# Chunked delta rule and token/channel mixer on one core: inversion rounds of two and then four units, and a first batch element ordered by hand

## The chip, the cores and the metric

The kernel runs on one core of a Trainium2 chip. The metric is the device time of one execution in microseconds; three executions before the change gave 915.23, 920.13 and 922.28 us. A difference of about 1% is what such a measurement can tell from none.

## The reference

Four batch elements, eight heads, 768 time steps, head size 48. A delta rule keeps a 48 x 48 state per head; its output, heads side by side, goes through an MLP mixer over tokens and one over channels. All is float32.

```python
k_n = k / (np.linalg.norm(k, axis=-1, keepdims=True) + 1e-06)
for t in range(S):
    y[:, :, t] = np.einsum('bhd,bhde->bhe', q[:, :, t], state)
    v_old = np.einsum('bhde,bhd->bhe', state, kt)
    state = state + bt[:, :, :, None] * np.einsum('bhd,bhe->bhde', kt, vt - v_old)
...
h = np.maximum(x.transpose(0, 2, 1) @ w_tok1, 0.0) @ w_tok2      # x: (4, 768, 384)
u = x + h.transpose(0, 2, 1)
out = u + np.maximum(u @ w_ch1, 0.0) @ w_ch2
```

The inputs arrive as 64-bit floats where numpy made them so (the four weights); the kernel turns these into float32 itself.

## The kernel before, in words

**Units.** A unit is 128 time steps of one batch element, all eight heads; there are 24, six to a batch element. Inside a unit the time steps are two chunks of C = 64. For a chunk the sequential rule becomes matrix algebra: with a strictly triangular matrix N of k-products times beta, the inverse of a unit triangular 64 x 64 matrix is needed per chunk and head. A unit therefore has 16 such matrices, and each is handled as two 32 x 32 diagonal blocks and one off-diagonal block.

**The stages of a unit.** `load_kq` (L213) brings k and q. `prep` (L246) normalises k (ScalarE square L255, VectorE L257 to L271), restacks it with four transfers into kst (L278), transposes k and q on TensorE (L286, L299), spreads them into the block-diagonal kbd (ScalarE L291, GpSimd L292), multiplies p_g (L310, sixteen matmul records a unit) and masks it into gm on VectorE (L312, twice a unit); the diagonal 32 x 32 blocks then go to DRAM (L327). `invert` (L333) works on a round of RU = 2 units: it loads their 64 diagonal blocks one to a partition (L339), runs the substitution as 30 pairs of VectorE operations (L344, L348), makes a transposed copy xt on GpSimd (L355), stores both to DRAM (L358, L359) and fetches them back in the layout of matmul operands: wt (L369), w22 (L373) and t11 (L378). `join` (L384) makes the off-diagonal block with two rounds of matmuls, p_z (L392) and p_x (L403). `recur` (L412) is one chunk of the recurrence, a step: p_q (L427), r_bd on VectorE (L429, two operations), p_w (L442), w_bd on ScalarE (L446), p_s (L451), the state s_bd on VectorE (L455, two operations) and the output chunk y (L433, L461). The state chains one step to the next; a batch element has twelve steps.

**The mixer.** `mixer` (L468) of a batch element needs all six units of it, as the token MLP sums over time: p_1 (L475), then p_h (L487), and then per 128 time steps p_c (L513) and p_o (L528) of the channel MLP. TensorE is free to work on the next batch element's units between these.

**The weights.** `round_weights` (L159) takes a piece of up to 384 columns: one load of 64-bit words (L168), two ScalarE operations (L174, L175), two integer VectorE operations (L176, L180), one on GpSimd (L184), and one on VectorE (L186) for the result. There are 34 pieces: ten of w1 and w2, then twelve each of wc1 and wc2. `beta` is read with sixteen small transfers (L144) and transposed.

**Order.** Nothing is written out by hand: each stage is a generator, `at(time, dt, fn, ...)` (L544) gives it a due time and a step, in units of one unit's work, and `run_plan` (L547) calls the generators in the order of due times. That order is a priority: the scheduler that builds each engine's fixed instruction list may put an operation that it expects to be ready ahead of an older one that it expects to wait. Each engine then runs its own list strictly in order. All transfers are issued from SyncE's queue, also in order.

```python
at(t0 - 2.9 + j, 0.08, prep, u)
if j == 0:
    at(t0 - 1.4, 0.9 / (HB + 2), invert, rnd)
at(t0 - 0.4 + 0.2 * j, 0.1, join, u)
for cc in range(2):
    at(u + 0.5 * cc, 0.15, recur, 2 * u + cc)
if c == NCH - 1:
    at(u + 1, NCH / (n_mixer + 1), mixer, b)
```

The functions, with the line numbers of the profile:

## Time and profile before

| | |
|---|---|
| median of three runs | 920.13 us (915.23 to 922.28) |
| profiled execution | 917.84 us, span 916.1 us, granted TensorE clock 0.901 in the mean |
| busy share of the span | PE 80%, PE weight load 65%, VectorE 52%, ScalarE 25%, GpSimd 15% |
| transfers | 56.06 MB, 28.8% of 16 engines' span on the one queue that carries them |

All times in rows are of the one profiled execution. PE is TensorE's matmuls and PEld its weight loads, DVE is VectorE, ACT ScalarE, POOL GpSimd, SP SyncE and SPq its queue of transfers. A granted clock of 1 is 2.4 GHz, of 0.5 is 1.2 GHz. A float32 matmul of the program appears as two matmul records.

### The profile page before, as it was taken

How to read it: one execution, taken by the hardware profiler on the slowest of the kernel's cores; microseconds unless marked ns; L12 is line 12 of the kernel's file. 1: busy time of each engine (PE TensorE's matmuls, PEld its weight loads, DVE VectorE, ACT ScalarE, POOL GpSimd, SP SyncE). 2: the span in 40 equal slices, each digit the busy share in tenths (PEclk: the TensorE clock that was granted, in tenths of full speed). 3: DMA queues.
4: the chain of work that ended last, by engine and by line, in shares of the span. 5: the costliest groups of instructions: out<-in, count | busy, mean ns of one | idle time of the engine just before them, and what ended most of it. 6: DMA issues, size and time to landing. Idle time of an engine off the chain costs nothing.

```text
span 916.1 us, 13640 instructions
## 1 busy us (share of the span) xinstructions
PE 735.6 (80%) x5034; PEld 594.5 (65%) x5034; DVE 473.3 (52%) x1254; ACT 232.5 (25%) x535; POOL 138.3 (15%) x150
## 2 busy tenths in 40 slices
PE   3301820660889999999899999998999999799998
PEld 2301710540758878877688788786888787567876
DVE  5696499285274491763835918548358174210000
ACT  3322523320311412313124133041241321211110
POOL 7433225120110100201101012011011000000000
PEclk9555875695699999999999999999999999989999
DMA  5655444431232322413223234232230212000000
GB/s 105 139 134 121 92 110 134 99 74 37 41 61 44 66 49 55 95 44 63 59 56 60 42 74 79 48 73 41 56 67 21 50 38 54 11 1 9 18 9 18
DMA packets 192354, 56.06 MB, mean 61 GB/s; under 512 B 182560, under 2 KB 185632, under 8 KB 192288
## 3 DMA queue, kind: packets, MB, share of 16 engines
q1 hardware_dynamic: 192288, 55.19, 28.8%
q8 instruction: 40, 0.66, 0.3%
q14 instruction: 26, 0.21, 0.1%
HBM read 36.27 MB, written 14.16 MB: 55 GB/s over the span
## 4 chain that ended last, share of the span: by engine, by line
PE 58%; DVE 19%; DMA 7%; ACT 5%; issue 4%; POOL 3%; SPq 3%; POOLq 0%; ACTq 0%; DVEq 0%
PE p_c L513 14%; PE p_o L528 13%; DVE x L348 6%; DVE sub L344 6%; PE p_s L451 6%; PE p_q L427 4%; PE p_w L442 4%; PE p_h L487 4%; PE p_g L310 3%; PE p_z L392 3%; PE p L475 3%; PE p_x L403 3%; ACT w_bd L446 3%; DMA t_dram<-xt 2%; DMA t<-t_dram 1%
## 5 line engine op out<-in xcount | busy, mean ns | idle before, releaser
L513 PE MATMUL p_c<-u_t,wc 128*128 128x128 f32 x1728 | 202.6, 276 | 2.3 <-ACT u_t L501 2.3
L513 PEld LDWEIGHTS p_c<-u_t,wc 128*128 128x128 f32 x1728 | 198.3, 192 | 7.7 <-ACT u_t L501 3.2
L528 PE MATMUL p_o<-wc,r 128*128 128x384 f32 x576 | 196.7, 488 | 0.0
L528 PEld LDWEIGHTS p_o<-wc,r 128*128 128x128 f32 x576 | 104.8, 190 | 60.4
L392 PE MATMUL p_z<-t,gm 128*65 128x64 f32 x384 | 31.9, 246 | 122.2 <-DMA t<-t_dram 122.2
L348 DVE TENSOR_TENSOR x<-x,sub 64x30 f32<-64x30 f32 (+4 forms) x360 | 124.1, 345 | 9.9
L344 DVE TENSOR_TENSOR sub<-x 64x30 f32<-64x30 f32 (+4 forms) x360 | 120.3, 334 | 16.8 <-DMA x<-n_dram 7.6
L392 PEld LDWEIGHTS p_z<-t,gm 128*65 128x65 f32 x384 | 30.4, 162 | 127.3 <-DMA t<-t_dram 70.8
L520 ACT ACTIVATE r<-p_c 128x512 f32<-128x512 f32 x72 | 42.9, 596 | 242.9 <-PE p_c L513 242.8
L455 DVE TENSOR_TENSOR s_bd<-s_bd,p_s 64x192 f32<-64x192 f32 x80 | 28.5, 357 | 135.3 <-PE p_s L451 134.0
L535 DVE TENSOR_TENSOR o_sb<-p_o,xb 128x384 f32<-128x384 f32 x24 | 13.3, 556 | 132.7 <-PE p_o L528 132.4
L451 PE MATMUL p_s<-w_bd,gm 128*128 128x96 f32 x384 | 58.8, 296 | 11.1 <-ACT w_bd L446 8.6
L451 PEld LDWEIGHTS p_s<-w_bd,gm 128*128 128x128 f32 x384 | 50.5, 203 | 22.8 <-ACT w_bd L446 22.8
L310 PE MATMUL p_g<-kqt,kbd 128*128 128x128 f32 x384 | 56.8, 297 | 6.9 <-POOL kbd L292 4.7
L310 PEld LDWEIGHTS p_g<-kqt,kbd 128*128 128x128 f32 x384 | 51.1, 208 | 13.5 <-POOL kbd L292 13.3
L355 POOL COPY xt<-x 64x1024 f32<-64x1024 f32 x12 | 23.7, 1979 | 231.8 <-DVE x L348 231.8
L427 PEld LDWEIGHTS p_q<-s_bd,kqt 128*128 128x128 f32 x352 | 44.3, 194 | 17.9 <-DVE s_bd L455 5.7
L427 PE MATMUL p_q<-s_bd,kqt 128*128 128x96 f32 x352 | 49.8, 282 | 7.2 <-DVE s_bd L455 7.0
L429 DVE TENSOR_TENSOR r_bd<-v_st,p_q 64x192 f32<-64x192 f32 x88 | 31.4, 357 | 31.9 <-PE p_q L427 24.0
L433 ACT ACTIVATE xb<-p_q 64x384 f32<-64x384 f32 x44 | 21.2, 483 | 103.1 <-DVE r_bd L429 100.5
L442 PE MATMUL p_w<-r_bd,wt 128*65 128x96 f32 x384 | 43.2, 257 | 5.0 <-DVE r_bd L429 2.5
L292 POOL COPY kbd<-kqt 64x512 f32<-64x512 f32 x24 | 16.3, 678 | 202.9 <-ACT kqt L290 202.1
(68 smaller groups left out, 743.4 us busy)
## 6 DMA issues: line engine op xcount, KB each, us to landing
d<-in_moe_w_ch_dram SPq DMA_DIRECT2D x24, 384.0 KB
kpad<-in_k_dram SPq DMA_DIRECT2D x24, 192.0 KB
qpad<-in_q_dram SPq DMA_DIRECT2D x24, 192.0 KB
kst<-kpad SPq DMA_DIRECT2D x96, 48.0 KB
v_st<-in_v_dram SPq DMA_DIRECT2D x96, 48.0 KB
out_dram<-o_sb SPq DMA_DIRECT2D x24, 192.0 KB
n_dram<-gm SPq DMA_DIRECT2D x96, 32.0 KB
x<-n_dram SPq DMA_DIRECT2D x12, 256.0 KB
```

What stands on the lines that cost most here:

```text
L310: nc.tensor.matmul(p_g[:, i], kbd[0][:, nb], kqt[:, nb])
L344: nc.vector.tensor_tensor(out=tmp, in0=x[:, 0:s, s : s + 1].to_broadcast([n, s, w]), in1=x[:, s : s + 1, s + 1 : HB].to_broadcast([n, s, w ...
L348: nc.vector.tensor_tensor(out=x[:, 0:s, s + 1 : HB], in0=x[:, 0:s, s + 1 : HB], in1=tmp, op=ALU.add,)
L392: nc.tensor.matmul(p_z[0:65, nb], gm[:, lo : lo + 65], t11[:, nb])
L427: nc.tensor.matmul(p_q[:, p], kqt[:, 2 * p + cc], s0[:, p])
L429: nc.vector.tensor_tensor(out=r_bd[r, :, e], in0=v_st[r, :, cc], in1=p_q[hi, :, e], op=ALU.subtract,)
L442: nc.tensor.matmul(p_w[0 : C + 1, p], wts[u % NV][:, w_lo : w_lo + C + 1], r_bd[:, p])
L451: nc.tensor.matmul(p_s[:, p], gm[:, 2 * p + cc, 0:2], w_bd[:, p])
L487: nc.tensor.matmul(p_h, w2[:, j, c * 128 : (c + 1) * 128], r1[j], start=(j == 0), stop=(j == NDH - 1),)
L513: nc.tensor.matmul(p_c[:, i], wc1[:, cb, f * 128 : (f + 1) * 128], u_t[:, cb], start=(cb == 0), stop=(cb == NCB - 1),)
L520: nc.scalar.activation(r, p_c, ACTF.Relu)
L528: nc.tensor.matmul(p_o, r2[f // FG][:, f % FG], wc2[:, f], start=(f == 0), stop=(f == NHT - 1),)
```

## The change

`RU` becomes 4, and the rounds are [0, 1], [2 to 5], [6 to 9] and so on, with [22, 23] last; a round of four holds 128 blocks. The transposed copy xt moves from GpSimd to ScalarE. Fetching is a function of its own, `fetch_w`, called unit by unit; w22 is gone, since p_x now takes the second column half of wt (32 columns instead of 64) with a wider zst. gm and kqt have six buffers, wt has three, x has one. The four kst transfers and a single transfer for beta are issued from ScalarE's queue, beta's transpose becomes 24 small matmuls, and k and q of unit u + 2 are loaded by `prep(u)`. The mask product mb moves to `prep`'s second step. For batch element 0 `recur` works on two halves of the head pairs, the second with the mixer's PSUM buffers. A weight piece is loaded two pieces ahead of its rounding, with three load buffers, and the scaled low words overwrite the low words. The mixer's p_1 runs over time first with two accumulators; the last sum is written into xb, and r2 has four buffers. The due times of rounds 0 and 1, of the fetches and of the weights are set separately. The core of the diff:

```diff
-RU = 2
+RU = 4
...
-    NV = 4
+    NV = 6
...
-    wts = zeroed("wt", [128, NB * C + 8], NV, nc.gpsimd)
+    NW = 3
+    wts = zeroed("wt", [128, NB * C + 8], NW, nc.gpsimd)
...
+
+        rows = mlp_pool.tile([B * H, S], FP32, name="b_rows", tag="xb")
+        nc.scalar.dma_start(out=rows, in_=beta.rearrange("b h s -> (b h) s"))
+        yield
+        p_b = ps_prep([128, NQ, B * NP], "p_b")
+        for c in range(NQ):
+            for par in range(2):
+                nc.tensor.matmul(
+                    p_b[C * par : C * par + C, c], rows[:, c * C : (c + 1) * C],
+                    ident[: B * H, par : B * H : 2],
+                )
+        nc.scalar.copy(beta_st.rearrange("s b p c -> s c (b p)"), p_b)
+        yield
 
...
-        d64 = loads.tile([128, n], mybir.dt.int64, name="d64")
+        d64 = loads.tile([128, WP], mybir.dt.int64, name="d64", bufs=3)[:, 0:n]
         nc.sync.dma_start(out=d64, in_=src)
+        yield
...
+    def load_weights(*pairs):
+
+        pieces = []
+        for dst, src in pairs:
...
+                    pieces.append(round_weights(dst[:, j, cut], rows[j, :, cut]))
+        n = len(pieces)
+        for i in range(n + 2 + 1):
+            for lag in (2 + 1, 2, 0):
+                if 0 <= i - lag < n:
+                    next(pieces[i - lag], None)
+            yield
...
+    xouts = {}
+    rounds = [[0, 1], [2, 3, 4, 5]]
+    while rounds[-1][-1] < NU - 1:
+        u = rounds[-1][-1] + 1
+        rounds.append(list(range(u, min(u + RU, NU))))
+    round_of = {u: (r, j) for r, us in enumerate(rounds) for j, u in enumerate(us)}
...
-                nc.sync.dma_start(
+                nc.scalar.dma_start(
                     out=kst[C * par : C * par + C, :, cc],
                     in_=kp[C * cc : C * cc + C, par::2, 0:D],
                 )
...
+        assert not turning
+        turning.add(u)
+        mb = work.tile([128, NP, 2, C], FP32, name="mb", bufs=1)
+        nc.gpsimd.tensor_tensor(
+            out=mb, in0=mask_c[:, None, None, :].to_broadcast([128, NP, 2, C]),
+            in1=bet[:, :, :, None].to_broadcast([128, NP, 2, C]), op=ALU.mult,
+        )
...
+        if u + 2 < NU:
+            load_kq(u + 2)
...
-        n_dram = xins.pop(rnd)
-        n = n_dram.shape[0]
-        x = work.tile([n, HB, HB], FP32, name="x")
-        nc.sync.dma_start(out=x, in_=n_dram)
+        n = 4 * NB * len(rounds[rnd])
+        x = work.tile([RU * 4 * NB, HB, HB], FP32, name="x", bufs=1)[0:n]
+        nc.sync.dma_start(out=x, in_=xins.pop(rnd)[0:n])
...
-        nc.gpsimd.tensor_copy(out=xt, in_=x.rearrange("b s t -> b t s"))
...
+        xt = work.tile([RU * 4 * NB, HB, HB], FP32, name="xt", bufs=1)[0:n]
+        nc.scalar.copy(xt, x.rearrange("b s t -> b t s"))
+        w_dram = dram.tile([RU * 4 * NB, HB, HB], FP32, name="w_dram")
+        t_dram = dram.tile([RU * 4 * NB, HB, HB], FP32, name="t_dram")
+        nc.sync.dma_start(out=w_dram[0:n], in_=x)
+        nc.sync.dma_start(out=t_dram[0:n], in_=xt)
+        xouts[rnd] = (w_dram, t_dram)
+        yield
...
+    def fetch_w(u):
+        assert u < NW or u - NW in walked
+        rnd, j = round_of[u]
+        w_dram, t_dram = xouts[rnd]
+        wt = wt_of(u)
+        for par in range(2):
+            for i in range(2):
+                lo = (4 * j + 2 * par + i) * NB
+                row = C * par + HB * i
+                nc.sync.dma_start(
+                    out=wt[row : row + HB, :, HB * i : HB * i + HB],
+                    in_=w_dram[lo : lo + NB].rearrange("b s t -> s b t"),
+                )
+                if i == 0:
                     nc.sync.dma_start(
-                        out=wt[row : row + HB, :, HB * i : HB * i + HB], in_=x_s
+                        out=t11s[u % 2][row : row + HB, :, HB * par : HB * par + HB],
+                        in_=t_dram[lo : lo + NB].rearrange("b s t -> s b t"),
                     )
...
+        p_x = ps_prep([128, NB, HB], "p_x")
+        for nb in range(NB):
+            lo = nb * 2 * HB
+            nc.tensor.matmul(
+                p_x[0:65, nb], zst[:, lo : lo + 65], wt[:, nb, HB : 2 * HB]
             )
...
+
+        halves = ((0, NP // 2), (NP // 2, NP)) if b == 0 else ((0, NP),)
+        ps = [ps_seq, ps_mlp]
+
+        for i, (p0, p1) in enumerate(halves):
+            hp = slice(p0, p1)
+            if c > 0:
+                p_q = ps[i]([128, NP, 2 * D], "p_q")
+                for p in range(p0, p1):
+                    nc.tensor.matmul(p_q[:, p], kqt[:, 2 * p + cc], s0[:, p])
+                for r, e in heads:
+                    nc.vector.tensor_tensor(
+                        out=r_bd[r, hp, e], in0=v_st[r, hp, cc], in1=p_q[hi, hp, e],
+                        op=ALU.subtract,
+                    )
+                nc.scalar.mul(y[:, hp], p_q[lo, hp], -1.0)
...
+
+        for i, (p0, p1) in enumerate(halves):
+            hp = slice(p0, p1)
+            p_w = ps[i]([128, NP, 2 * D], "p_w")
+            for p in range(p0, p1):
+                w_lo = (2 * p + cc) * C
+                nc.tensor.matmul(
+                    p_w[0 : C + 1, p], wts[u % NW][:, w_lo : w_lo + C + 1], r_bd[:, p]
+                )
             for r, e in heads:
+                nc.scalar.copy(w_bd[r, hp, e], p_w[lo, hp, e])
...
+        late = []
+        for i, (p0, p1) in enumerate(halves):
+            hp = slice(p0, p1)
+            p_s = ps[i]([128, NP, 2 * D], "p_s")
+            for p in range(p0, p1):
+                nc.tensor.matmul(p_s[:, p], gm[:, 2 * p + cc, 0:2], w_bd[:, p])
...
+        for hp, p_s in late:
...
+        p_1 = [ps_mlp([128, DM], "p_1") for _ in range(NDH)]
+        for c in range(NCH):
+            for dh in range(NDH):
+                nc.tensor.matmul(
+                    p_1[dh], w1[:, c, dh * 128 : (dh + 1) * 128], xb[:, c],
+                    start=(c == 0), stop=(c == NCH - 1),
+                )
+            yield
...
-    n_mixer = 3 * NDH + NCH + NCH * (1 + NHT + NHT // 2)
-    at(-4, 0, load_beta)
+    n_mixer = NCH + NCH + NCH * (1 + NHT + NHT // 2)
+    at(-9, 5, load_beta)
+    for rnd, us in enumerate(rounds):
+        t0 = us[0]
+        for j, u in enumerate(us):
+            if rnd == 0:
+                t_prep = -3.0 + 0.25 * j
+            elif rnd == 1:
+                t_prep = -2.35 + 0.35 * j
+            else:
+                t_prep = max(t0 - 3.0 + 0.3 * j, u - NV + 1 + 0.01)
+            if u < 2:
+                at(-9, 0, load_kq, u)
+            at(t_prep, 0.06, prep, u)
+            at(t0 - 0.45 + 0.75 * j, 0, fetch_w, u)
+            at(t0 - 0.3 + 0.75 * j, 0.1, join, u)
+        if rnd == 0:
+            at(-2.4, 2.0 / (HB + 2), invert, rnd)
+        elif rnd == 1:
+            at(-0.45, 1.9 / (HB + 2), invert, rnd)
+        else:
+            at(t0 - 1.55, 0.95 / (HB + 2), invert, rnd)
     for u in range(NU):
-        rnd, j = divmod(u, RU)
-        t0 = RU * rnd
         b, c = divmod(u, NCH)
-        at(t0 - 3.6 + j, 0, load_kq, u)
-        at(t0 - 2.9 + j, 0.08, prep, u)
-        if j == 0:
-            at(t0 - 1.4, 0.9 / (HB + 2), invert, rnd)
         at(u - 0.9, 0, load_v, u)
-        at(t0 - 0.4 + 0.2 * j, 0.1, join, u)
         for cc in range(2):
             at(u + 0.5 * cc, 0.15, recur, 2 * u + cc)
         if c == NCH - 1:
             at(u + 1, NCH / (n_mixer + 1), mixer, b)
-    n_pieces = sum(t.shape[1] * -(-t.shape[2] // WP) for t in (w1, w2, wc1, wc2))
-    at(-1.9, (NCH + 2.6) / (n_pieces + 1), load_weights)
+    at(-3.5, 0.3, load_weights, (w1, moe_w_tok1), (w2, moe_w_tok2))
+    at(1.0, 0.2, load_weights, (wc1, moe_w_ch1), (wc2, moe_w_ch2))
```

## Rows read from the trace of the kernel before

**Rows 1.** Page, the span in 40 equal slices: TensorE's busy tenths.
```profile
PE   3301820660889999999899999998999999799998
```
**Rows 2.** Busy time by stage: stage, length; per engine busy (instructions); clock, DMA share, GB/s.
```profile
0.00:262.00 262.00, 103.16 (x710) 88.46 (x710) 170.57 (x414) 78.03 (x179) 82.50 (x94) 0.69 0.44 98
36.00:87.00 51.00, 0.57 (x3) 0.29 (x3) 45.16 (x110) 13.66 (x30) 19.91 (x17) 0.50 0.61 142
...
262.00:916.00 654.00, 632.41 (x4324) 506.01 (x4324) 302.69 (x841) 154.43 (x356) 55.80 (x57) 0.99 0.23 46
```
**Rows 3.** Waits, 0 to 262 us: us in total, times, longest.
```profile
PE p_z L392 <- DMA t<-t_dram: 120.1, 3, 50.4
```
**Rows 4.** Timeline of TensorE where p_h starts: start, length, engine, line.
```profile
264.34 8.74 PE L487 MATMUL p_h<-r,w 128*128 128x384 f32 x24
```
**Rows 5.** Page, costliest groups: count, busy us, mean ns, idle before.
```profile
L348 DVE TENSOR_TENSOR x<-x,sub 64x30 f32<-64x30 f32 (+4 forms) x360 | 124.1, 345 | 9.9
L344 DVE TENSOR_TENSOR sub<-x 64x30 f32<-64x30 f32 (+4 forms) x360 | 120.3, 334 | 16.8 <-DMA x<-n_dram 7.6
```
**Rows 6.** Groups by line with shapes kept apart, whole span; columns as in rows 5.
```profile
L310 PE MATMUL p_g<-kqt,kbd 128*128 128x128 f32 x384 | 56.8, 297 | 6.9 <-POOL kbd L292 4.7 <-ACT kqt L300 2.1
...
L312 DVE TENSOR_TENSOR gm<-p_g,mb 128x512 f32<-128x512 f32 x48 | 32.6, 685 | 24.0 <-PE p_g L310 18.3 <-issue 4.3 <-POOL gm L301 0.8
...
L429 DVE TENSOR_TENSOR r_bd<-v_st,p_q 64x192 f32<-64x192 f32 x88 | 31.4, 357 | 31.9 <-PE p_q L427 24.0 <-issue 4.9
...
L455 DVE TENSOR_TENSOR s_bd<-s_bd,p_s 64x192 f32<-64x192 f32 x80 | 28.5, 357 | 135.3 <-PE p_s L451 134.0
...
L461 DVE TENSOR_TENSOR xb<-xb,p_s 64x384 f32<-64x384 f32 x44 | 24.1, 548 | 7.1 <-PE p_s L451 5.8
...
L186 DVE SCALAR_TENSOR_TENSOR wc<-w_a,w_f 128x384 f32<-128x384 f32 x24 | 16.7, 697 | 9.6 <-POOL w_f L184 9.6
L271 DVE TENSOR_TENSOR kpad<-kpad,krec 128x384 f32<-128x384 f32 x24 | 16.7, 694 | 0.6
...
L535 DVE TENSOR_TENSOR o_sb<-p_o,xb 128x384 f32<-128x384 f32 x24 | 13.3, 556 | 132.7 <-PE p_o L528 132.4
...
L257 DVE TENSOR_REDUCE ksum<-ksq 128x8 f32<-128x384 f32 x24 | 13.0, 543 | 6.6 <-ACT ksq L255 6.5
...
L344 DVE TENSOR_TENSOR sub<-x 64x240 f32<-64x240 f32 x24 | 9.6, 400 | 0.8
...
L344 DVE TENSOR_TENSOR sub<-x 64x30 f32<-64x30 f32 x24 | 4.8, 200 | 8.1 <-DMA x<-n_dram 7.6
```
**Rows 7.** Stage 0 to 262 us, instructions on d alone: VectorE busy, ScalarE busy.
```profile
0.00:262.00 262.00, 36.45 (x68) 32.44 (x68) 0.69 0.44 98
```
**Rows 8.** Timeline of the first substitution and its hand-off: start, length, engine, line.
```profile
36.67 0.18 DVE L344 TENSOR_TENSOR sub<-x 64x30 f32<-64x30 f32 x1 [3.66 <-DMA x<-n_dram]
...
78.07 1.99 POOL L355 COPY xt<-x 64x1024 f32<-64x1024 f32 x1 [1.48 <-DVE x L348]
78.30 2.19 DVE L180 SCALAR_TENSOR_TENSOR w_f<-d,w_f 128x384 uint32<-128x384 uint32 x1
...
87.02 1.99 PE L392 MATMUL p_z<-t,gm 128*65 128x64 f32 x16 [50.45 <-DMA t<-t_dram]
```
**Rows 9.** Timeline, SyncE's queue at the start: issue begins, time of all issues.
```profile
0.74 6.53 SPq L144 DMA_DIRECT2D b_rows<-in_beta_dram  x16
```
**Rows 10.** Timeline, SyncE's queue: the issues of one unit's kst.
```profile
14.48 2.68 SPq L278 DMA_DIRECT2D kst<-kpad  x4
```
**Rows 11.** Timeline of TensorE: the first p_w, and two neighbouring p_q of batch element 0.
```profile
92.74 1.51 PE L442 MATMUL p_w<-r_bd,wt 128*65 128x96 f32 x8 [0.87 <-issue]
...
108.55 1.13 PE L427 MATMUL p_q<-s_bd,kqt 128*128 128x96 f32 x8 [0.76 <-DVE s_bd L455]
...
114.23 1.10 PE L427 MATMUL p_q<-s_bd,kqt 128*128 128x96 f32 x8
```

More of the change, by code (lines that the diff above doesn't have):

```diff
@@ L342, in invert @@
             w = HB - 1 - s
-            tmp = work.tile([n, s, w], FP32, name="sub")
+            tmp = work.tile([RU * 4 * NB, HB * HB // 4], FP32, name="sub")
+            tmp = tmp[0:n, 0 : s * w].rearrange("b (s w) -> b s w", w=w)
             nc.vector.tensor_tensor(
@@ L392, in join @@
             nc.tensor.matmul(p_z[0:65, nb], gm[:, lo : lo + 65], t11[:, nb])
-        z = zst[:, 0 : NB * HB].rearrange("s (b n) -> s b n", n=HB)
+        z = zst[:, 0 : NB * 2 * HB].rearrange("s (b n) -> s b n", n=2 * HB)
         for par in range(2):
-            row = C * par + HB
-            nc.scalar.copy(
-                z[row : row + HB], p_z[HB : 2 * HB, :, HB * par : HB * par + HB]
-            )
-        yield
-        p_x = ps_prep([128, NB, 2 * HB], "p_x")
-        for nb in range(NB):
-            lo = nb * HB
-            nc.tensor.matmul(p_x[0:65, nb], zst[:, lo : lo + 65], w22[:, nb])
+            row, e = C * par + HB, slice(HB * par, HB * par + HB)
+            nc.scalar.copy(z[row : row + HB, :, e], p_z[HB : 2 * HB, :, e])
+        yield
[4 more added lines that the diff above has]
+                p_x[0:65, nb], zst[:, lo : lo + 65], wt[:, nb, HB : 2 * HB]
+            )
         for par in range(2):
@@ L406, in join @@
             nc.scalar.copy(
-                wt[row : row + HB, :, HB : 2 * HB],
-                p_x[0:HB, :, HB * par : HB * par + HB],
+                wt[row : row + HB, :, HB : 2 * HB], p_x[HB * par : HB * par + HB]
             )
@@ L417, in recur @@
         if c == 0:
-            xbs[b] = mlp_pool.tile([128, NCH, DM], FP32, name="xb")
+            xbs[b] = mlp_pool.tile([128, NCH, DM], FP32, name="xb", tag="xb")
         xb = xbs[b]
@@ L423, in recur @@
         y = xb[C * cc : C * cc + C, c // 2].rearrange("s (p n) -> s p n", p=NP)
-        if c > 0:
-            p_q = ps_seq([128, NP, 2 * D], "p_q")
-            for p in range(NP):
-                nc.tensor.matmul(p_q[:, p], kqt[:, 2 * p + cc], s0[:, p])
-            for r, e in heads:
+        halves = ((0, NP // 2), (NP // 2, NP)) if b == 0 else ((0, NP),)
[13 more added lines that the diff above has]
+            else:
+                for r, e in heads:
+                    nc.gpsimd.tensor_copy(out=r_bd[r, hp, e], in_=v_st[r, hp, cc])
@@ L429, in recur @@
+        for hp, p_s in late:
+            if c > 0:
                 nc.vector.tensor_tensor(
-                    out=r_bd[r, :, e], in0=v_st[r, :, cc], in1=p_q[hi, :, e],
-                    op=ALU.subtract,
-                )
-            nc.scalar.mul(y, p_q[lo], -1.0)
-        else:
-            for r, e in heads:
-                nc.gpsimd.tensor_copy(out=r_bd[r, :, e], in_=v_st[r, :, cc])
-        yield
-        p_w = ps_seq([128, NP, 2 * D], "p_w")
-        for p in range(NP):
-            w_lo = (2 * p + cc) * C
-            nc.tensor.matmul(
-                p_w[0 : C + 1, p], wts[u % NV][:, w_lo : w_lo + C + 1], r_bd[:, p]
-            )
@@ L445, in recur @@
-        for r, e in heads:
-            nc.scalar.copy(w_bd[r, :, e], p_w[lo, :, e])
-        yield
-        p_s = ps_seq([128, NP, 2 * D], "p_s")
-        for p in range(NP):
-            nc.tensor.matmul(p_s[:, p], gm[:, 2 * p + cc, 0:2], w_bd[:, p])
-        if c < NQ - 1:
-            for r, e in heads:
-                if c > 0:
-                    nc.vector.tensor_tensor(
-                        out=s1[r, :, e], in0=s0[r, :, e], in1=p_s[hi, :, e], op=ALU.add
-                    )
-                else:
-                    nc.vector.tensor_copy(out=s1[r, :, e], in_=p_s[hi, :, e])
@@ L460, in recur @@
-        if c > 0:
-            nc.vector.tensor_tensor(out=y, in0=y, in1=p_s[lo], op=ALU.add)
-        else:
-            nc.scalar.copy(y, p_s[lo])
+                    out=y[:, hp], in0=y[:, hp], in1=p_s[lo, hp], op=ALU.add
+                )
+            else:
+                nc.scalar.copy(y[:, hp], p_s[lo, hp])
         if cc == 1:
@@ L470, in mixer @@
         xb = xbs[b]
+        p_1 = [ps_mlp([128, DM], "p_1") for _ in range(NDH)]
[4 more added lines that the diff above has]
+                    start=(c == 0), stop=(c == NCH - 1),
+                )
+            yield
         r1 = []
         for dh in range(NDH):
-            p_1 = ps_mlp([128, DM], "p_1")
-            for c in range(NCH):
-                nc.tensor.matmul(
-                    p_1, w1[:, c, dh * 128 : (dh + 1) * 128], xb[:, c],
-                    start=(c == 0), stop=(c == NCH - 1),
-                )
-                if c % 2:
-                    yield
             r = mlp_pool.tile([128, DM], FP32, name="r1")
-            nc.scalar.activation(r, p_1, ACTF.Relu)
+            nc.scalar.activation(r, p_1[dh], ACTF.Relu)
             r1.append(r)
```

102 lines of the change are left out of this document (25 added, 77 removed).

## The prediction

> **What bounds the kernel now.** I read the page's slices of the span first, then the busy time by stage, then the waits of the first stage, then single stretches of the timeline. In the slices [rows 1] the reader sees two kernels in one: eleven slices in which TensorE is often idle, and then a row of eights and nines to the end. The stages [rows 2] put numbers on it. From 262 us on TensorE is busy for 632.4 of 654 us at a granted clock of 0.99: a bound that this change does not move, since the mixer's matmuls, and those of the units still to come, stay as they are but for one width. Before 262 us it is busy for 103.2 of 262 us, and 120.1 us of the rest are three waits for one thing [rows 3]: p_z, the first matmul of a join, waits for the transfer that brings the inverted blocks back. There is one such wait per round of two units, and batch element 0, whose six units must all be through before its mixer can sum over the sequence, has three rounds in a row. The mixer's second stage, p_h, starts at 264.3 us [rows 4]; from there to the end of the span are 916.1 - 264.3 = 651.8 us. So the forecast is the new start of p_h, plus what follows it.
>
> In that first stage VectorE is the busiest engine: 170.6 of 262 us [rows 2]. What fills it can be rebuilt from the groups. One round of substitution is (124.1 + 120.3) / 12 = 20.4 us [rows 5]. A unit's preparation is 2 x 0.685 + 0.543 + 0.694 = 2.6 us [rows 6]. Of the weights' rounding, the two integer operations of all 34 pieces are 36.5 us [rows 7], and the last one 0.697 us each [rows 6], together 60.2 us or 1.77 us a piece. A recurrence step is 4 x 0.357 + 0.548 = 1.98 us [rows 6]. Three rounds, nine units prepared by then, 34 pieces and 12 steps: 61.1 + 23.5 + 60.2 + 23.7 = 168.5 us against 170.6 measured. The 2.1 us left are the zero fills and small operations. The sum holds, so I use it for the new kernel.
>
> **The change part by part.**
>
> *Rounds of two, then four.* Units 2 to 5 share one substitution on 128 partitions where two ran on 64. A VectorE operation costs by its elements in a partition: 64x384 takes 548 ns and 128x384 takes 556 ns [rows 6]. So a round of four costs 20.4 us as well; bounds 20.4 and, if partitions did count, 40.8. Over the kernel seven rounds replace twelve, 5 x 20.4 = 102 us less on VectorE. Most of that falls after 262 us, where VectorE works 302.7 of 654 us beside a TensorE that is full [rows 2], and is worth nothing there. What counts is that batch element 0 has two hand-offs instead of three. A hand-off now runs from the end of the substitution, 78.07 us, to the first p_z, 87.02 us: 9.0 us [rows 8]. I keep 9.0: the transposing copy moves to ScalarE, whose price for it the trace does not show (from nothing to twice GpSimd's 1.99 us); a fetch for one unit is shorter than for two; a round of four stores twice the bytes.
>
> *The start.* The sixteen transfers for beta hold SyncE's queue for 6.5 us ahead of everything else [rows 9]; now one on ScalarE's queue replaces them, and k comes first. The first substitution starts at 36.7 us now [rows 8]. I take 31 (bounds 30 and 36.7; against it stand two more buffers to clear on GpSimd).
>
> *kst on ScalarE's queue.* Four issues cost SyncE 2.7 us a unit [rows 10]. The same on ScalarE is not in the trace: between nothing and 2.7 us plus the wait for the normalised k, in a queue where the kbd copies and w_bd stand behind it. I take 2.7 us hidden: ScalarE is busy for 154.4 of 654 us [rows 2]. The Trainium skill speaks against much of a gain ("DMA: Bandwidth & Descriptors", Issuing engines are not separate DMA queues): issuing from several engines saves only the sequencer's issue time, usually small beside the transfer. Here that time is not small, 0.7 us for one kst [rows 10]; by the rule the move gives 0, by the row at most 2.7 us once, ahead of the first load of x. My sum holds neither.
>
> *Two halves of a step, for batch element 0.* A step now takes 5.7 us, from p_q at 108.55 to p_q at 114.23 [rows 11], with 1.98 us of VectorE in it: a chain of PE, VectorE, PE, ScalarE, PE, VectorE in which each waits for the last. Two independent halves overlap. The price is twice the VectorE instructions. Length costs (400 - 200) / (240 - 30) = 0.95 ns an element [rows 6], so a piece of 96 elements costs 357 - 96 x 0.95 = 266 ns, and half of the sum for y 548 - 192 x 0.95 = 365 ns: 8 x 0.266 + 2 x 0.365 = 2.86 us a step, 0.9 more. The period of a step must lie between this 2.86 (VectorE alone) and today's 5.7; half-way is 4.3. The Trainium skill prices a piece lower ("VectorE: DVE Perf Modes", The TRN2 errata: 120 cycles plus the elements at 0.96 GHz for a PSUM source), as an estimate 225 ns, which would take 12 x 8 x 0.04 = 4 us off VectorE's sum; for 192 elements it says 325 ns where the trace has 357, so I stay with the rows.
>
> *Weights.* Loads run two pieces ahead with three buffers. No VectorE work goes; what goes is its standing in a queue behind a tile that has not landed. In 36 to 87 us VectorE is busy 45.2 of 51 us, 0.885 [rows 2]. I take 0.92 for the new first stage (bounds 0.885 and 1). One GpSimd operation less, the copy xt, also helps: beside it an operation of VectorE took 2.19 us [rows 8]; that is 1.5 us a round at most, and not in the sum.
>
> *Small edits*, at nothing: p_x with 32 columns instead of 64, the mixer's p_1 in another order, o_sb gone, NW = 3. They lie in stages full of other work or change only buffers; bounds -3 and +3 us together.
>
> **The sum.** First the chain. Substitution 0 from 31, with the preparation of units 2 to 5 (10.4 us) and some three weight pieces (5.3 us) among it: (20.4 + 10.4 + 5.3) / 0.92 = 39 us, so 70. Hand-off 9: p_z at 79, and from p_z to the first p_w another 5.7 us (87.02 to 92.74) [rows 8, 11]. The second x is loaded meanwhile; substitution 1 with steps 0 to 3: (20.4 + 4 x 2.86) / 0.92 = 35 us, 114. Hand-off and join, 14.7: 128.5. Eight steps of 4.3: 163. About 2 us for the last of p_1: 165. Nothing else may delay it for that.
>
> Now VectorE. Until p_h starts it has two or three substitutions, ten preparations, 34 pieces, 12 steps: 61.2 + 26 + 60.2 + 34.3 + 2.1 = 184 us with three. Some 14 of them lie before 31 us (fills, two preparations, four pieces), and the last four pieces (7 us) may come later, since wc2 is used last: 163 us remain, 143 without the third substitution (units 6 to 9), which batch element 0 does not need. At 0.92 these take 177 or 155 us: 208 or 186, and with 2 us for p_1, 210 or 188. VectorE binds, not the chain. I take 188: the third substitution's due times, from 4.45 on, lie behind most steps' and ahead of the last two only.
>
> After p_h starts: 651.8 us less the matmuls p_g of one more unit prepared early, 56.8 / 24 = 2.4 us [rows 6], so 649.4. Span 188 + 649.4 = 837.4; around the span lie 917.84 - 916.1 = 1.7 us; execution 839 us. It is measured against the profiled 917.84; the median of the runs shown is 920.13, 0.25% above, so the gain, 79 us or 8.6%, is the same against either.
>
> **The rivals.**
> 1. *The chain sets the time.* If the scheduler leaves the roundings to VectorE's gaps, p_h starts at 165: 165 + 649.4 + 1.7 = 816. For it: a step needs 2.9 of 4.3 us of VectorE, and the two hand-offs leave 30 us of gaps. Against: the sum of 143 us has to go somewhere, and the weights' due times lie among the steps'. Chance 0.17.
> 2. *The third substitution goes ahead and nothing runs denser*: 163 / 0.885 = 184, p_h at 217, 868. For it: its due times precede steps 10 and 11. Against: its data must first be prepared. Chance 0.16.
> 3. *The change doesn't do what it says but for the count of rounds*: halves no faster, start no earlier; one of three waits goes, 120.1 / 3 = 40 us: 878. Against: the chain is plainly serial in rows 11. Chance 0.05.
> 4. *Rounds of four bring the hand-off back into the full stage*: five later rounds, each with 9.0 us of TensorE waiting, 839 + 45 = 884. Against: the due times leave three times the room between the end of a substitution and its join. Chance 0.04.
> 5. *Slower: ScalarE's queue.* The four kst issues wait there for VectorE's normalised k, then take 2.7 us, and w_bd and the mixer's activations stand behind them; TensorE runs in order and stops. It decides from (917.8 - 839) / 18 = 4.4 us lost per later unit. With 2.7 us and a wait of as much, 5.4 x 18 = 97: 936. For it: ScalarE is in every step's chain. Against: it has three quarters of its time free [rows 2], and TensorE has the other batch element's matmuls ahead. Chance 0.05.
>
> **How the numbers follow.** The forecast has 0.53; its own range is 825 to 855. The range for 8 in 10 reaches to the chain's 816 less 10 for a shorter step (4.3 down to 3.1 for eight steps), 806, and up to the cases 2 and 3, 878. Faster by over 1%: all but rivals 5 and a part of what no rival names, 0.93; within 1%, which is about what a measurement of this kernel can tell from no change, 0.02; slower 0.05.
>
> **What would show it.** Right: p_h starts near 188 us; two waits of p_z for t_dram before it, not three; substitution 0 starts near 31; steps of batch element 0 some 4 us apart where VectorE is free; VectorE busy near 0.9 up to p_h; L344 and L348 near 210 instances each with the same means; from p_h to the end about 649 us. Wrong: means that grow with the partitions; ScalarE's kst issues ahead of w_bd with TensorE idle behind them; long waits of p_z after p_h; a p_h before 170 (rival 1) or after 210 (rival 2).

## The result, and the profile after

The changed kernel takes 863.36 us (median of four, 862.48 to 865.15) against 920.36 for the kernel before on the same chip: a ratio of 0.939, 95% interval 0.936 to 0.943. The profiled execution is 862.48 us, its span 860.7. The forecast was 839, with 806 to 878 as range.

Below: the page's slices of the changed kernel, then its busy time by stage (columns as in [rows 2]).

```profile
PE   4551272787869999999999999999999999999998
...
PEclk9755565696779999999999999999999999999999
```
```profile
0.00:231.00 231.00, 127.43 (x785) 110.57 (x786) 153.77 (x407) 85.92 (x219) 74.84 (x91) 0.67 0.51 112
231.00:860.70 629.70, 610.27 (x4296) 501.34 (x4295) 232.44 (x598) 164.71 (x360) 38.49 (x49) 0.99 0.21 45
105.70:134.90 29.20, 21.38 (x121) 18.36 (x121) 21.88 (x70) 11.16 (x35) 1.97 (x2) 0.62 0.24 60
154.60:221.00 66.40, 55.05 (x408) 50.70 (x408) 34.97 (x102) 27.90 (x86) 11.43 (x13) 0.76 0.46 94
```

The same two kernels in one as in [rows 1], but the full stage begins earlier, at p_h. [rows 2] split the kernel before at 262 us; split at its own p_h, 264.3 us, what lies behind is:

```profile
264.34:916.10 651.76, 630.16 (x4321) 504.85 (x4319) 300.41 (x832) 153.73 (x354) 55.45 (x56) 0.99 0.23 46
```

Taken as TensorE's busy plus idle time, the gain is nearly all idle time ahead of p_h: 159 us idle there before (264.3 less 105.4 busy), 231 - 127.4 = 104 now. Behind p_h the idle time is 22 and 19 us. TensorE's busy time in the two stages together hardly moved (735.6 and 737.7), but 22 us more of it lie ahead of p_h and 20 us less behind. So p_h came only 33.5 us sooner than in [rows 4], and the rest of the gain shows behind it.

The waits of TensorE for the hand-off, 0 to 262 us, answer to [rows 3]: two now, not three.

```profile
PE p_z L393 <- DMA t<-t_dram: 47.3, 2, 29.9
```

The substitution's groups of the page answer to [rows 5]:

```profile
L347 DVE TENSOR_TENSOR sub<-x 128x84 f32<-128x84 f32 (+22 forms) x210 | 75.6, 360 | 13.7 <-DMA x<-n_dram 8.7
L351 DVE TENSOR_TENSOR x<-x,sub 128x84 f32<-128x84 f32 (+22 forms) x210 | 75.3, 359 | 5.2
```
The same groups with shapes kept apart; one shape of each kernel can be compared, 64x240 in [rows 6] and here:
```profile
L347 DVE TENSOR_TENSOR sub<-x 128x240 f32<-128x240 f32 x10 | 4.1, 406 | 0.3
```

Next, TensorE, then ScalarE and its queue (ACT, ACTq) and then VectorE in the timeline just ahead of the first substitution, whose x was issued at 34.38 us:

```profile
39.95 1.09 PE L286 MATMUL p_t<-ident,kpad 128*128 128x128 f32 x4 [5.74 <-DVE kpad L264]
```
```profile
39.88 2.92 ACTq L271 DMA_DIRECT2D kst<-kpad  x4
42.84 0.59 ACT L290 COPY kqt<-p_t 128x512 f32<-128x512 f32 x1 [4.36 <-DMA kst<-kpad]
43.33 0.58 ACT L291 COPY kbd<-p_t 64x512 f32<-64x512 f32 x1
43.80 0.59 ACT L300 ACTIVATE kqt<-p_t 128x512 f32<-128x512 f32 x1
44.30 0.52 ACT L253 ACTIVATE ksq<-kpad 128x384 f32<-128x384 f32 x1
```
```profile
39.25 0.56 DVE L264 TENSOR_TENSOR kpad<-kpad,krec 128x384 f32<-128x384 f32 x1
44.84 0.55 DVE L255 TENSOR_REDUCE ksum<-ksq 128x8 f32<-128x384 f32 x1 [5.03 <-ACT ksq L253]
46.70 0.69 DVE L314 TENSOR_TENSOR gm<-p_g,mb 128x512 f32<-128x512 f32 x1 [1.30 <-PE p_g L312]
47.31 0.17 DVE L347 TENSOR_TENSOR sub<-x 64x30 f32<-64x30 f32 x1
```

Read it from the bottom. The substitution does not wait for its own data here; it stands on VectorE behind a gm (L314), which waits 1.30 us for p_g, and a ksum (L255) of another unit, which waits 5.03 us for ksq, and ksq stands on ScalarE behind three copies that stood behind the four kst issues. Between the 39.8 at which VectorE ended L264 and 47.3 it did 1.2 us of work. The issues are not all of the wait: the first copy reads p_t, which TensorE ended at 41.0, and started at 42.8, so they held it for 1.8 us.

The rest of the chain, on ScalarE and TensorE:

```profile
91.66 2.00 ACT L358 COPY xt<-x 64x1024 f32<-64x1024 f32 x1 [0.94 <-DVE x L351]
```
```profile
100.08 1.99 PE L393 MATMUL p_z<-t,gm 128*65 128x64 f32 x16 [29.91 <-DMA t<-t_dram]
...
105.70 1.54 PE L450 MATMUL p_w<-r_bd,wt 128*65 128x96 f32 x8 [0.82 <-ACT wt L407]
...
134.90 2.32 PE L433 MATMUL p_q<-s_bd,kqt 128*128 128x96 f32 x8
154.64 2.02 PE L393 MATMUL p_z<-t,gm 128*65 128x64 f32 x16 [17.42 <-DMA t<-t_dram]
...
230.79 4.14 PE L503 MATMUL p_h<-r,w 128*128 128x384 f32 x12
242.68 1.01 PE L503 MATMUL p_h<-r,w 128*128 128x384 f32 x1 [7.75 <-DVE xb L507]
```

From the first p_w to the p_q of step 4, four steps (and one join among them) take 29.2 us, 7.3 each, at a granted clock of 0.62 by the stages above, a mean between the two levels.

### The profile page after: what moved, and what is told of

It is laid out like the page before. It is cut to its first block, busy times and chain, and to the rows that moved or that the text cites. A ratio compares the mean times of both kernels' runs of the same rounds, so it can differ in the third digit from the quotient of the medians.

```text
span 860.7 us, 13445 instructions
## 1 busy us (share of the span) xinstructions
PE 737.7 (86%) x5080; PEld 611.9 (71%) x5080; DVE 386.2 (45%) x1004; ACT 250.6 (29%) x578; POOL 113.3 (13%) x139
## 4 chain that ended last, share of the span: by engine, by line
PE 66%; DVE 14%; ACT 4%; issue 3%; DMA 3%; POOL 1%; ACTq 1%; SPq 0%; POOLq 0%; DVEq 0%
PE p_c L529 18%; PE p_o L544 18%; PE p_s L462 5%; DVE sub L347 4%; DVE x L351 4%; PE p_q L433 4%; PE p_h L503 4%; PE p_g L312 3%; PE p_w L450 3%; PE p_z L393 3%; PE p_x L402 3%; PE p L490 3%; DVE r_bd L435 1%; DVE s_bd L466 1%; DMA t_dram<-xt 1%
## 5 line engine op out<-in xcount | busy, mean ns | idle before, releaser
L529 PE MATMUL p_c<-u_t,wc 128*128 128x128 f32 x1728 | 212.4, 277 | 1.3 <-ACT u_t L517 1.3
L347 DVE TENSOR_TENSOR sub<-x 128x84 f32<-128x84 f32 (+22 forms) x210 | 75.6, 360 | 13.7 <-DMA x<-n_dram 8.7
L351 DVE TENSOR_TENSOR x<-x,sub 128x84 f32<-128x84 f32 (+22 forms) x210 | 75.3, 359 | 5.2
L466 DVE TENSOR_TENSOR s_bd<-s_bd,p_s 64x192 f32<-64x192 f32 (+1 forms) x100 | 31.6, 316 | 99.0 <-PE p_s L462 97.0
L550 DVE TENSOR_TENSOR xb<-xb,p_o 128x384 f32<-128x384 f32 x24 | 13.2, 551 | 134.5 <-PE p_o L544 134.4
L393 PE MATMUL p_z<-t,gm 128*65 128x64 f32 x384 | 31.3, 242 | 47.3 <-DMA t<-t_dram 47.3
L312 PEld LDWEIGHTS p_g<-kqt,kbd 128*128 128x128 f32 x384 | 56.1, 226 | 20.1 <-POOL kbd L292 17.6
L435 DVE TENSOR_TENSOR r_bd<-v_st,p_q 64x192 f32<-64x192 f32 (+1 forms) x110 | 34.8, 317 | 50.8 <-PE p_q L433 48.2
L439 ACT ACTIVATE xb<-p_q 64x384 f32<-64x384 f32 (+1 forms) x55 | 22.9, 419 | 118.4 <-DVE r_bd L435 112.3
L450 PE MATMUL p_w<-r_bd,wt 128*65 128x96 f32 x384 | 45.6, 263 | 11.7 <-DVE r_bd L435 8.2
L314 DVE TENSOR_TENSOR gm<-p_g,mb 128x512 f32<-128x512 f32 x48 | 32.9, 688 | 41.0 <-PE p_g L312 40.3
L450 PEld LDWEIGHTS p_w<-r_bd,wt 128*65 128x65 f32 x384 | 38.8, 149 | 16.9 <-issue 6.0
```

What stands on the lines that cost most here:

```text
L312: nc.tensor.matmul(p_g[:, i], kbd[0][:, nb], kqt[:, nb])
L347: nc.vector.tensor_tensor(out=tmp, in0=x[:, 0:s, s : s + 1].to_broadcast([n, s, w]), in1=x[:, s : s + 1, s + 1 : HB].to_broadcast([n, s, w ...
L351: nc.vector.tensor_tensor(out=x[:, 0:s, s + 1 : HB], in0=x[:, 0:s, s + 1 : HB], in1=tmp, op=ALU.add,)
L393: nc.tensor.matmul(p_z[0:65, nb], gm[:, lo : lo + 65], t11[:, nb])
L435: nc.vector.tensor_tensor(out=r_bd[r, hp, e], in0=v_st[r, hp, cc], in1=p_q[hi, hp, e], op=ALU.subtract,)
L450: nc.tensor.matmul(p_w[0 : C + 1, p], wts[u % NW][:, w_lo : w_lo + C + 1], r_bd[:, p])
```

## The experiments

All ratios are against the kernel before; the changed kernel is 0.939 [0.936, 0.943].

**Whole steps.** The halves are undone.
```diff
-        halves = ((0, NP // 2), (NP // 2, NP)) if b == 0 else ((0, NP),)
+        halves = ((0, NP),)
```


> Batch element 0 back to whole steps, all else as changed (863.4 us, p_h from 230.8 us, TensorE's granted clock 0.59 in 100 to 136 us). Clock theory: two halves spread TensorE's matmuls thin, its clock stays at the lower level, and at that level the matmuls of a step alone take 6.4 us; whole steps bring the clock in the first recurrence to about 0.85 and the step to some 5.8 us, so the time falls by 5 to 20 us. Chain theory (the forecast's): halves shorten a step by 1.4 us, so undoing them costs 8 to 17 us. VectorE theory: 0.9 us less VectorE work a step, 11 us in all, so the time falls by up to 11 us with the clock as it was.

857.75 us, ratio 0.939 [0.935, 0.943]: the same. The clock from 100 to 136 us is 0.59 as with halves, so the halves are not what holds it down, and they are worth nothing that can be measured in the end. The zero is the sum of two effects. With whole steps the second p_z comes 62.8 us after the first, with halves 54.6; p_h then comes 65.2 us after it, with halves 76.2. What ends the stage differs, first in the changed kernel, then in this run:
```profile
221.17 9.68 PE L490 MATMUL p<-xb,w 128*128 128x384 f32 x24
```
```profile
225.14 2.19 PE L490 MATMUL p<-xb,w 128*128 128x384 f32 x4 [0.71 <-DVE xb L475]
```
With whole steps 20 of p_1's 24 matmul records run among the steps and 2.2 us of it are left; with halves, whose second half uses the mixer's PSUM buffers, all 24 come behind the last step. That the buffers are the reason is argued, not shown by an edit of their own. In return more of the weights' rounding stands ahead of the second p_z with whole steps (VectorE's operations on w_f take 17.3 us between the two p_z, 10.0 with halves).

**kst on SyncE's queue.**
```diff
-                nc.scalar.dma_start(
+                nc.sync.dma_start(
                     out=kst[C * par : C * par + C, :, cc],
```


> The four kst transfers of a unit back on SyncE's queue, all else as changed. ScalarE-queue theory: substitution 0 starts at 47.3 us instead of 31 because ScalarE's in-order queue stops behind the kst issues (three waits, 18.3 us) and VectorE then waits for ScalarE's square of k; on SyncE it starts by 40 us or earlier and the time falls by 7 to 15 us. Rival: SyncE's queue is the tighter one (n_dram, loads of k, q, x and weights stand in it), so substitution 0 starts no earlier and the time is the same or up to 10 us more.

849.95 us, ratio 0.928 [0.923, 0.933]: about 1.2% less than the changed kernel by the ratios. VectorE's timeline and TensorE's p_z of this run:
```profile
36.36 0.56 DVE L264 TENSOR_TENSOR kpad<-kpad,krec 128x384 f32<-128x384 f32 x1
40.11 0.18 DVE L347 TENSOR_TENSOR sub<-x 64x30 f32<-64x30 f32 x1 [3.19 <-DMA x<-n_dram]
```
```profile
88.30 1.99 PE L393 MATMUL p_z<-t,gm 128*65 128x64 f32 x16 [15.01 <-DMA t<-t_dram]
...
142.72 2.02 PE L393 MATMUL p_z<-t,gm 128*65 128x64 f32 x16 [17.40 <-DMA t<-t_dram]
```
Now the substitution waits for x and nothing else. It starts 7.2 us earlier, both p_z 12 us, p_h 13 (at 217.7). That is more than the issues' own time: the edit also changed the fixed order, and here the substitution stands right behind L264, ahead of the next unit's ksum and gm. The substitution is shorter, too: from its first operation to xt it takes 38.7 us where the changed kernel takes 44.4. This holds for all kernels tried, 37.9 to 39.6 us in the seven with kst on SyncE's queue, 43.9 to 45.6 in the six with kst on ScalarE's. The start is a weaker reading, as it moves from profile to profile: 39.9 to 47.7 us in the seven, 46.8 to 51.6 in the six.

**Both.** The two diffs above in one kernel.

> Edit: both earlier edits together, whole steps for batch element 0 and the kst transfers on SyncE's queue. Theory A (the two are independent: the halves are worth nothing, the queue about 10 us): 845 to 852 us, the first p_z near 88 us, p_h near 215 us. Theory B (halves pay once the chain starts earlier): 854 to 862 us, the time between the first p_z and p_h longer than the 129 us that the halved kernel with kst on SyncE's queue had.

849.16 us, 0.927 [0.922, 0.931], first p_z 88.06, p_h 218.07: the queue's gain, and nothing from the halves again. The two effects are there again: 62.9 us between the two p_z (54.4 with halves), 67.1 from the second to p_h (75.0).

**Rounds of two.** All other parts of the change stay.
```diff
-RU = 4
+RU = 2
-    rounds = [[0, 1], [2, 3, 4, 5]]
+    rounds = [[0, 1]]
```


> Rounds of two units throughout, with the new due times, queues and halves. If the sharing of a substitution by four units is what gained, batch element 0 has three hand-offs again and p_h starts 25 to 40 us later: 885 to 905 us, and VectorE is busy about 100 us more over the span. If the due times and the loads made ahead are what gained, the loss is under 10 us.

887.1 us, 0.967 [0.963, 0.972]. Three hand-offs are back; TensorE's timeline:
```profile
105.89 1.99 PE L393 MATMUL p_z<-t,gm 128*65 128x64 f32 x16 [53.44 <-DMA t<-t_dram]
...
157.70 2.02 PE L393 MATMUL p_z<-t,gm 128*65 128x64 f32 x16 [14.32 <-DMA wt<-w_dram]
...
220.08 1.99 PE L393 MATMUL p_z<-t,gm 128*65 128x64 f32 x16 [26.22 <-DMA t<-t_dram]
...
263.09 7.36 PE L503 MATMUL p_h<-r,w 128*128 128x384 f32 x22
```
So the rounds of four are worth some 24 us of the 57. They bring p_h 32 us sooner (230.8, 263.1 here) and lose 9 us behind it (629.9, here 884.2 - 263.1 = 621), where the changed kernel has the wait of 7.75 us in the middle of p_h shown above and this run has none. On VectorE they save 482.8 - 386.2 = 96.6 us. The other 33 us come with the other edits: against the kernel before p_h is 1 us sooner (264.3) and 31 us less lie behind it (651.8). Taken as TensorE's time these are 12 us less idle ahead of p_h, 9 us less idle behind it and 11 us less busy (724.6 against 735.6).

**Old order of p_1.** The mixer's first product loops over output blocks first, each with one accumulator, as before.
```diff
-        for c in range(NCH):
-            for dh in range(NDH):
+        for dh in range(NDH):
+            p_1 = ps_mlp([128, DM], "p_1")
+            for c in range(NCH):
```


> The mixer's p_1 in its old order (one accumulator at a time, two time blocks to a step of the plan), all else as changed. In the changed kernel all 24 p_1 matmuls of batch element 0 run after the last step, 221.2 to 230.8 us; before, 17 of 24 ran in gaps of the recurrence. If the pair of accumulators held up the filling (both halves of the steps use the same PSUM buffers), p_h starts 4 to 8 us earlier and the time falls by as much. Rival: the fill is held up by the halves' use of those buffers alone, and nothing changes (within 2 us).

861.53 us, 0.941 [0.937, 0.945]: the same. The order of p_1 is thus not what keeps it behind the last step.

**Weight loads beside their rounding.**
```diff
-        for i in range(n + 2 + 1):
-            for lag in (2 + 1, 2, 0):
+        for i in range(n + 1):
+            for lag in (1, 0, 0):
```


> Edit to the changed kernel alone: a weight piece is loaded in the same step as its rounding again, as before the change (kst stays on ScalarE's queue). Changed kernel: 863.36 us. With rounds of two, all else as changed, the time was 887.1, so the other edits together are worth some 30 us. Theory A (loads ahead of their rounding are the main part of those 30): 875 us or more, with VectorE and ScalarE waiting for d. Theory B (they are worth little, as the fixed order of each engine is built with the transfer's time in it): 858 to 868 us.

855.56 us, 0.933 [0.929, 0.937]: not slower. Loading ahead is not where the 33 us are.

**Old due times for the last round.** Units 22 and 23 only.
```diff
+            elif rnd == len(rounds) - 1:
+                t_prep = t0 - 2.9 + j
...
+            at(t0 - 1.4, 0.9 / (HB + 2), invert, rnd)
```


> Edit to the changed kernel alone: the last round (units 22 and 23) gets the due times of before again (preparation 2.9 before the unit, one unit apart, substitution 1.4 before). Open question: after p_h the changed kernel needs 629.9 us where the kernel before needed 651.8. In the trace of before the last four steps stand alone behind the mixer of batch element 2 (from 773.7 to 803 us), in the changed one they lie among its matmuls. Theory A (the due times of the last round put them there): the steps stand alone again, 875 to 885 us, some 15 to 20 us more, the last p_s followed by p_1 behind an idle TensorE. Theory B (the order follows from something else, such as rounds that are shorter on VectorE): 858 to 868 us.

867.61 us, 0.945 [0.940, 0.949]: the same within the intervals. The last steps of the whole kernel still lie among the mixer's matmuls, as the timelines of TensorE show, first of the kernel before, then of this run:
```profile
796.22 1.10 PE L427 MATMUL p_q<-s_bd,kqt 128*128 128x96 f32 x8 [0.93 <-DVE s_bd L455]
798.25 1.28 PE L442 MATMUL p_w<-r_bd,wt 128*65 128x96 f32 x8 [0.93 <-DVE r_bd L429]
800.32 2.02 PE L451 MATMUL p_s<-w_bd,gm 128*128 128x96 f32 x8 [0.79 <-ACT w_bd L446]
803.06 2.93 PE L475 MATMUL p<-xb,w 128*128 128x384 f32 x4 [0.71 <-DVE xb L461]
```
```profile
738.25 2.20 PE L529 MATMUL p_c<-u_t,wc 128*128 128x128 f32 x18
740.29 0.82 PE L450 MATMUL p_w<-r_bd,wt 128*65 128x96 f32 x8
740.95 4.06 PE L544 MATMUL p_o<-wc,r 128*128 128x384 f32 x12
744.85 1.03 PE L462 MATMUL p_s<-w_bd,gm 128*128 128x96 f32 x8
745.71 4.06 PE L544 MATMUL p_o<-wc,r 128*128 128x384 f32 x12
749.61 7.90 PE L490 MATMUL p<-xb,w 128*128 128x384 f32 x24
```
In the kernel before, the last steps have no other matmul beside them but those of two joins and p_1; the products shown wait for VectorE or ScalarE, and from 773.7 to 805.8 us TensorE does four steps, two joins and p_1, busy for 25.5 of the 32.1 us. Which edit ended that stays open: undoing the rounds, p_1's order or the last round's due times, one at a time, leaves the last steps among the mixer's matmuls.

**Matmuls that nobody reads.** On top of kst on SyncE's queue, one after each substitution step of rounds 0 and 1.
```diff
+            if rnd < 2:
+                p_f = ps_mlp([128, DM], "p_f")
+                cols = DM if rnd == 0 else 256
+                nc.tensor.matmul(p_f[:, 0:cols], ident, warm[:, 0:cols])
```


> Edit: kst on SyncE's queue, and besides one matmul of ident by zeros after each substitution step of rounds 0 and 1 (384 columns in round 0, 256 in round 1), whose result nobody reads. Base without it: 849.95 us, granted clock 0.58 from 100 to 143 us, p_h at 217.7 us. Theory A (TensorE's low clock stretches the steps, and through VectorE's in-order queue the substitution beside them): the clock of that stretch rises to 0.85 or more, p_s of four from 1.17 to about 0.6 us, the second p_z comes 8 to 14 us sooner, 835 to 843 us. Theory B (waits between engines set the steps, not the length of the matmuls): clock up, time 846 to 854 us. Theory C (the extra matmuls stand in TensorE's in-order queue ahead of the steps): slower, over 855 us.

845.92 us, 0.923 [0.919, 0.927]; the kernel without them had 0.928 [0.923, 0.933], so the end shows no difference. Busy time from p_z to p_z, of the kernel without them and then with them:
```profile
88.00:142.00 54.00, 27.43 (x160) 24.05 (x160) 38.38 (x120) 18.79 (x49) 9.29 (x10) 0.56 0.40 102
```
```profile
93.00:141.00 48.00, 31.05 (x200) 26.33 (x200) 38.79 (x119) 18.45 (x49) 8.35 (x9) 0.75 0.43 115
```
The clock rises from 0.56 to 0.75, short of theory A's 0.85, and the stretch is 6 us shorter. The first p_z is at 93.16, not 88.30, which is not laid to the matmuls, as kernels without them have it anywhere from 88.1 to 95.4. From it to p_h are 125.1 us, 129.4 without them, so in these two profiles the later start takes back what the stretch gained; what 4 us would do to the time is below what the intervals can tell.

**Preparation of units 6 to 9 earlier, and later.** Both with kst on SyncE's queue. Earlier, into the second wait:
```diff
+            elif rnd == 2:
+                t_prep = max(1.2 + 0.3 * j, u - NV + 1 + 0.01)
```


> Edit: kst on SyncE's queue, and besides the due times of the preparation of round 2 (units 6 to 9) earlier, at 1.2 and on, as far as the buffers of gm allow. Base without it: 849.95 us, a wait of 17.4 us of TensorE for the second t_dram. Theory A (after the first p_z the kernel's time is TensorE's work plus its idle time, and work that is moved into the wait comes off the end): two preparations of some 3.3 us each at full clock fill the wait, 841 to 846 us. Theory B (the moved preparation stands ahead of the steps on TensorE and VectorE and pushes the second substitution back by as much): 848 to 856 us, second p_z later than 142.7 us.

845.68 us, 0.922 [0.918, 0.926]. The time is what theory A said. The second p_z is at 146.01, later than 142.72, but not for theory B's reason: the first is at 92.89 already, and between the two lie 53.1 us, 54.4 without this edit, with the p_t and p_g of one preparation (24 records) among them. p_h is at 219.2, no earlier, with more work done before it. Against the same kernel without this edit the intervals overlap, so theory A's gain is not shown. Later:
```diff
+                t_prep = 5.2 + 0.07 * j
...
+            at(t0 - 0.51, 0.03 / (HB + 2), invert, rnd)
```


> Edit: kst on SyncE's queue, and besides round 2 (units 6 to 9) gets due times behind those of nearly all steps of batch element 0 (preparation from 5.2, substitution from 5.49). Base without it: 849.95 us; from the second p_z (142.7 us) to p_h (217.7 us) 75 us, in which TensorE is busy 60 us, with four joins and four preparations beside the eight steps. Theory A (TensorE's and VectorE's work for units 6 to 9 stands among the steps and stretches them): the stretch falls to 50 to 62 us, p_h near 200 us; the time itself stays within 1% (846 to 856 us), since the work that is moved behind p_h lengthens a stage in which TensorE is full. Theory B (the steps' own chain sets the stretch): 70 to 76 us still.

845.25 us, 0.920 [0.915, 0.924]; the stretch from the second p_z (148.53) to p_h (221.21) is 72.7 us, theory B's number. The test is weaker than meant: only the last of the four preparations went behind the steps, three stayed among the last four of them. Within the run they differ. TensorE's timeline, the p_w of steps 4 and 8 and the last p_s:
```profile
154.18 1.54 PE L450 MATMUL p_w<-r_bd,wt 128*65 128x96 f32 x8 [0.82 <-ACT wt L407]
...
178.50 1.51 PE L450 MATMUL p_w<-r_bd,wt 128*65 128x96 f32 x8 [0.33 <-PE p_q L433]
...
211.70 1.03 PE L462 MATMUL p_s<-w_bd,gm 128*128 128x96 f32 x8
```
Steps 4 to 7, with two joins and no preparation among them, take 24.3 / 4 = 6.1 us each; steps 8 to 11, with one join and three preparations, (212.7 - 178.5) / 4 = 8.6. The clock does not explain it: it is 0.78 in the first stretch and 0.84 in the second. That speaks for theory A's mechanism, though its number did not come; how much of the 8.6 the preparations make was not separated.

**Edits joined.** kst on SyncE's queue, units 6 to 9 earlier and loads beside their rounding; the second kernel has the unread matmuls as well.

> Edit: three at once, kst on SyncE's queue, round 2's preparation from 1.2 on, and a weight piece loaded in the step of its rounding. Singly: 849.95, 845.68 (with the first), and 855.56 against 863.36 (alone). Theory A (each takes away idle time of its own before p_h): 836 to 842 us. Theory B (they compete for the same idle time): 844 to 850 us.

> Edit: as the one with three edits, and besides the unread matmuls after each substitution step of rounds 0 and 1. Theory A (a higher clock before p_h shortens what TensorE does there): 3 to 8 us less than without them, granted clock from 100 to 150 us 0.7 or more. Theory B (the stretch is set by waits, not by the length of matmuls): within 3 us of the kernel without them.

846.18 us, 0.924 [0.920, 0.928], and 847.94 us, 0.925 [0.921, 0.928]. Nothing adds up beyond the single edits: theory B both times. The clock of the hand-off to hand-off stretch is 0.60 without and 0.75 with the extra matmuls, and the time does not follow. The simplest of the fast versions is kst back on SyncE's queue; the variants on top of it lie between 845 and 850 us and can't be told apart by their intervals, except that the whole group is 1 to 2% below the changed kernel.

## Why the prediction was right or wrong

The direction and the mechanism hold: one hand-off of batch element 0 less, 210 instances of each half of the substitution, on twice the partitions. Their means, 360 and 359 ns, are 4 to 8% above the 334 and 345 of [rows 5], but not by the partitions: 128x240 takes 406 ns, 64x240 took 400 [rows 6]. The time came out 24 us above the forecast through two errors that partly cancel: p_h at 231, not 188 (+43), and 630 us behind it, not 649 (-20).

*The chain.* Its terms, forecast and measured: substitution 0 starts at 31 and 47.3 (+16); it lasts 39 and 44.4 to xt (+5); hand-off 9.0 and 8.4; from the first p_z to the second 44 and 54.6 (+11); the join and eight steps up to p_1 40 and 66.5 (+27); p_1 2 and 9.6 (+8). The sum, +66, takes the chain's 165 to 231. Two of the terms have a run beside them: with kst on SyncE's queue the substitution lasts 38.7, and with whole steps 2.2 us of p_1 are left.

*"VectorE binds, not the chain"* is the step that failed. VectorE was busy for 153.8 of 231 us, 0.67 and not 0.92, and 35 of 66.4 us in the last stretch. I divided a sum by a density of 0.92, as if its gaps could be filled; but every engine's order is fixed, and VectorE stood in it waiting. Its longest waits from 31 to 231 us (us in total, times, longest) are for TensorE and GpSimd:
```profile
DVE s_bd L466 <- PE p_s L462: 19.0, 13, 7.8
DVE wc L178 <- POOL w_f L176: 11.7, 11, 1.3
DVE gm L314 <- PE p_g L312: 9.8, 6, 5.1
```
Rival 1 had the right kind of bound, with terms that were too short. That 188 came nearer than 165 was luck of size. Rival 2's sign, a p_h after 210, came without its reason: of the third substitution only four of thirty pairs run ahead of p_h, from this one on:
```profile
225.05 0.18 DVE L347 TENSOR_TENSOR sub<-x 128x30 f32<-128x30 f32 x1
```
That 863 lies near that rival's 868 is chance.

*The start.* The bound of 36.7 from above was too low: I had put ScalarE's kst issues at "2.7 us hidden". With kst back on SyncE's queue the substitution starts 7.2 us earlier and is 5.7 us shorter, and 13 us by the medians come off the end. The kernel did not get slower by this, as in rival 5, since what stood still lay ahead of p_h and not in the full stage. By the Trainium skill ("DMA: Bandwidth & Descriptors", Issuing engines are not separate DMA queues) little is to be had from another issuing engine. The run agrees and goes further: the move to ScalarE cost about 1.2%. The 2.9 us of issues stop an engine that computes, 1.8 us in the chain shown; the rest comes with the order that was built around them, which no run separates.

Nor is 31 reached with kst on SyncE's queue (39.9 at the earliest). One thing there the prediction had named: GpSimd's clearing of buffers. In eleven of the thirteen profiles with this start one kden, a small operation of VectorE, ends with the last of GpSimd's fills. In the changed kernel it is the second unit's; in the run with the old order of p_1 it is the first unit's, and the substitution starts 4.3 us later (51.62), behind the same order on VectorE. First the first unit's kden in the changed kernel, then it and the last fill in that run:
```profile
8.01 0.64 DVE L261 TENSOR_SCALAR kden<-knrm 128x8 f32<-128x8 f32 x1 [1.11 <-ACT knrm L259]
```
```profile
7.87 6.25 DVE L261 TENSOR_SCALAR kden<-knrm 128x8 f32<-128x8 f32 x1 [0.98 <-ACT knrm L259]
...
13.57 0.52 POOL L108 MEMSET zst<- 128x520 f32 x1
```
That the fills hold it is read from these times alone; no run takes them away.

*Steps of 4.3 us.* They take 7.3 us ahead of the second p_z and (221 - 160.3) / 8 = 7.6 behind it. My 5.7 us [rows 11] was read in a stretch whose clock I did not look at: 1.00 from 108.5 to 114.3 us of the kernel before. Here it is 0.62 and 0.76. And the sum for the eight steps left out TensorE's own work, four joins and four preparations beside the steps, 55 of 66.4 us busy. That two halves overlap was argued from the serial chain in [rows 11]; whole steps gave the same time, in both pairs of runs. The price I had left out is p_1: halves keep it behind the last step. The size of a half's operation was right: 0.256 us for 96 elements where I had 0.266. The Trainium skill's row for a PSUM source ("VectorE: DVE Perf Modes", The TRN2 errata), as an estimate 0.225, was below the measured value.

*"A bound that this change does not move."* Behind p_h 20 us less TensorE work was left, where I had counted one unit's p_g, 2.4 us. About 5 us are p_g and p_t of that unit. By groups the three products of the steps are 7 us shorter and p_1 6 us, its mean having fallen from 540 to 490 ns, but p_c is 10 us longer; groups overlap one another, so this is no sum that explains the rest. It would fit the last steps no longer running by themselves, but no run shows it alone. I had read the full stage as one row of nines [rows 1] and not looked at its end.

*Right:* the cost of a round of four, the hand-off (8.4 and, from xt at 144.75 to p_z at 154.64, 9.9 against 9.0), p_z to p_w (5.6 against 5.7), small edits at nothing (p_1's order).
